# Loading the first batch's x a pair or two earlier, and taking its four differences one per pair

## Chip, cores, metric

One core of one Trainium2 chip. The time is the device time of an execution in microseconds (us). Executions of one kernel mostly agree within some 0.2% here (before: 904.19 to 905.55).

## The reference

Hash attention on (4, 8, 768, 64) inputs, then a feed-forward of 2048 with a learned leak:

```python
q_bucket = bucket(q @ proj > 0);  k_bucket = bucket(k @ proj > 0)
scores = where(q_bucket == k_bucket, q @ k.T / sqrt(D), -1e9)
attn = exp(scores - max);  attn /= sum(attn) + 1e-9
x = (attn @ v) -> (B*S, H*D)                # 3072 x 512
h = x @ w_in
out = (max(h, 0) + alpha * min(h, 0)) @ w_out
```

## The kernel before

The attention walks 16 pairs of heads (0 to 15, four to a batch). For each pair TensorE (PE) does the scores (twelve cells of six matmuls), the hash of the next pair, the turns of the pair after it (transposes of q and k), attend (weights times v) and the row sums. ScalarE (ACT) does the exponentials. VectorE (DVE) adds up the exponentials (accp, accd), divides, and rounds one piece of the weights after another in between. Each pair's x goes to DRAM. The products of the feed-forward need seven operands x0 to x6 of a batch: x0, x1, x2, x5 are loaded from DRAM, and x3, x4, x5, x6 are made as differences on DVE.

```python
def load_x(b, *ns):                       # ns: 0 -> x0, 1 -> x1, 2 -> x2, 3 -> x5
    ...
    pinned(b == 0, nc.sync.dma_start(t, x_s[b, ...]))

def sum_x(b, n, engine):                  # one difference, 128x768 fp32
    to, a, c = ((3, 5, 0), (5, 2, 5), (4, 2, 3), (6, 4, 1))[n]
    ...
    do(engine.tensor_tensor(x_m[b, to], x_m[b, a], x_m[b, c], op=ALU.subtract))

def divide(pi, between=lambda: None):
    ...
    for g in range(NCH):
        do(DVE.transpose(a[:, g], sums[pi][:, g, :HW2]))        # L800, st <- sm: frees the sums' PSUM
    do(DVE.tensor_scalar(r, ...)); do(DVE.reciprocal(...)) ...   # and four small copies on POOL
    between()                                                    # weight work and accp
    do(DVE.transpose(d, ...))                                    # dn
    do(DVE.scalar_tensor_tensor(x, av[pi], vsum[pi], d, ...))    # x: frees attend's PSUM
    nc.sync.dma_start(x_s[b, hp], x)

for pi in range(NPAIR):
    i = 2 * pi
    def weight_begin():
        weight_clamp(i); weight_parts(i); add_first(pi)          # add_first: accp
    scores(pi, ...)                                              # PE, ACT
    if pi: divide(pi - 1, weight_begin)
    ...                                                          # weight piece i
    add_third(pi); add_last(pi)                                  # accp, accd
    weight_parts(i + 1); weight_sum(i + 1); ...
    add_total(pi)                                                # accd complete
    weight_sums(2)
    ...                                                          # hash, turns
    attend(pi); totals(pi)                                       # PE; totals: sm <- accd
    ...
    if pi + 2 < NPAIR: load(pi + 2, "v")
    if pi in (9, 11, 15): load_w(...)
    if pi in (10, 12, 13):
        load_x(0, *{10: (0,), 12: (1, 3), 13: (2,)}[pi])
    if pi in (13, 14):
        for n in range(2):
            sum_x(0, 2 * pi - 26 + n, DVE)
```

Scores, hashes, turns and sums share three buffers in PSUM, the memory that PE writes its products to. `do` keeps the program's order on each engine; which buffer a tile gets is settled when the program is built, from a model of the times. What stands at the end of the loop's body (loads, differences) runs around the start of the next pair's scores: the differences of pair 13 delay pair 14.

Of the kernel before, what the change touches and what calls it, by code (L numbers as in the profile page):

```python
# [406 lines left out]
def fast_path(  # L407
# [35 lines left out]
    PE, DVE, ACT, POOL = nc.tensor, nc.vector, nc.scalar, nc.gpsimd  # L443
# [117 lines left out]
    def load_weight(i):  # L561
        if i < NW:
            i = order[i]
            raw[i] = pool.tile([P, 512], moe_w_in.dtype, name=f"raw{i}", tag="raw", bufs=3)
            nc.sync.dma_start(raw[i], piece(i))
# [17 lines left out]
    def weight_clamp(i):  # L583
        if i < NW:
            i = order[i]
            x = wx[i]
            do(DVE.tensor_scalar(x, x, HI_MIN, None, op0=ALU.max, op1=ALU.max, accum_out=wmax[:, i : i + 1]))

    def weight_parts(i):
        i = order[i]  # L590
        lo, hi = halves(i)
        x = wx[i]
        wr[i] = r = pool.tile([P, 512], F32, name=f"wr{i}", tag="wr", bufs=1)
        do(DVE.tensor_scalar(
            x.bitcast(U32), x.bitcast(U32), 3, 0xC0000000, op0=ALU.logical_shift_left, op1=ALU.bitwise_xor,
        ))
        do(DVE.tensor_scalar(r.bitcast(U32), x.bitcast(U32), 0x7F800000, None, op0=ALU.bitwise_and))
        do(DVE.scalar_tensor_tensor(r, lo, 2.0 ** -52, r, op0=ALU.mult, op1=ALU.mult))

    def weight_sum(i):  # L600


        i = order[i]
        lo, hi = halves(i)
        x, r = wx[i], wr[i]
        if i < HW:
            n, m = divmod(i, 4)
            if m == 0:
                wst[n] = pool.tile([P, NM, 4, P], F32, name=f"wsi{n}", tag="wsi")
            slot = (0, 5, 1, 2)[m]  # L610
            dst = wst[n][:, slot].rearrange("p i f -> p (i f)")
        else:
            n, m = divmod(i - HW, 2)
            if m == 0:
                wst[HW + n] = pool.tile([P, 4, DM // 2], F32, name=f"wso{n}", tag="wso")
            w = wst[HW + n]
            dst = w[:, 0:4:3] if m == 0 else w[:, 1:3]
        turned = i < HW and m == 3
        do(DVE.scalar_tensor_tensor(
            r, x, -1.0 if turned else 1.0, r, op0=ALU.mult, op1=ALU.subtract if turned else ALU.add,  # L620
        ))
        if i >= HW:
            hi, r = (t.rearrange("p (a f) -> p a f", a=2) for t in (hi, r))
        do(DVE.scalar_tensor_tensor(
            dst.bitcast(U32), hi, 0x80000000, r.bitcast(U32), op0=ALU.bitwise_and, op1=ALU.bitwise_xor,
        ))
# [99 lines left out]
    def scores(pi, cells):  # L726
        for kc, g in cells:
            sc = two_banks(f"sc{pi}_{kc}_{g}")
            ks = slice(kc * P, (kc + 1) * P)
            qs = slice(g * CW, (g + 1) * CW)  # L730
            for what, first in ((bits, True), (tr, False)):
                for s in range(2):
                    r = slice(D * s, D * s + D)
                    do(PE.matmul(  # L734
                        sc[:, s, :CW], what["k", pi][r, ks], what["q", pi][r, qs], start=first, stop=not first,
                    ))
            do(ACT.activation(pts[kc][:, g, :, :CW], sc[:, :, :CW], AF.Exp, scale=SCALE / DOWN))  # L737
# [5 lines left out]
    def add_first(pi):  # L743
        accp[pi] = pool.tile([P, 2 * NCH, CW], F32, name=f"accp{pi}", tag="accp", bufs=1)
        do(DVE.tensor_tensor(accp[pi], p(0), p(1), op=ALU.add))  # L745
        if pi:
            nc.gpsimd.dma_start(accp[pi][:, 2:], p(2)[:, 2:], accum_op=ALU.add)
# [6 lines left out]
    def add_third(pi):  # L754
        n = 2 if pi else 4
        do(DVE.tensor_tensor(accp[pi][:, :n], accp[pi][:, :n], p(2)[:, :n], op=ALU.add))

    def add_total(pi):
        do(DVE.tensor_tensor(accd[pi], accd[pi], accp[pi], op=ALU.add))  # L759
# [29 lines left out]
    def divide(pi, between=lambda: None):  # L789



        b, hp = pairs[pi]
        n = HW2 // 32
        a = pool.tile([P, NCH, HW2], F32, name=f"st{pi}", tag="st", bufs=1)
        r = pool.tile([P, NCH, n], F32, name=f"rc{pi}", tag="rc")
        rr = pool.tile([P, NCH, 2, n], F32, name=f"rr{pi}", tag="rr")
        d = pool.tile([P, NCH, CW], F32, name=f"dn{pi}", tag="dn", bufs=1)
        for g in range(NCH):
            do(DVE.transpose(a[:, g], sums[pi][:, g, :HW2]))  # L800
        do(DVE.tensor_scalar(r, a.rearrange("p g (n w) -> p g n w", w=32)[:, :, :, 0], S * EPS, None, op0=ALU.add))
        for h in range(2):
            do(DVE.reciprocal(rr[:, :, h], r))
        for q0 in (0, D):
            q1 = q0 + 32
            do(POOL.tensor_copy(rr[q0 : q0 + 32, :, 1], rr[q1 : q1 + 32, :, 1]))
            do(POOL.tensor_copy(rr[q1 : q1 + 32, :, 0], rr[q0 : q0 + 32, :, 0]))
        vsum[pi] = pool.tile([P, 1], F32, name=f"vs{pi}", tag="vs")
        do(DVE.tensor_scalar(vsum[pi], av[pi][:, 0, CW : CW + 1], EPS, None, op0=ALU.mult))
        between()  # L810
        do(DVE.transpose(
            d.rearrange("p g w -> p (g w)"),
            rr.rearrange("p g h n -> p (g h n)").unsqueeze(2).to_broadcast([P, 2 * NCH * n, 32]),
        ))

        x = mid.tile([P, NCH, CW], F32, name=f"x{pi}", tag="x", bufs=1)
        do(DVE.scalar_tensor_tensor(x, av[pi][:, :, :CW], vsum[pi], d, op0=ALU.add, op1=ALU.mult))
        nc.sync.dma_start(x_s[b, hp], x.rearrange("p g w -> p (g w)"))
# [4 lines left out]
    def pinned(when, ins):  # L823

        if when:
            do(ins)

    def load_x(b, *ns):
        for n in ns or range(4):
            m, kh, ch = ((0, 0, 0), (1, 1, 0), (2, 1, 1), (5, 0, 1))[n]  # L830
            t = mid.tile([P, 2, CW], F32, name=f"x{b}_{m}", tag=f"x{m}", bufs=1)
            pinned(b == 0, nc.sync.dma_start(
                t, x_s[b, 2 * kh : 2 * kh + 2].rearrange("k p s -> p k s")[:, :, ch * CW : (ch + 1) * CW],
            ))
            x_m[b, m] = t

    def sum_x(b, n, engine):

        to, a, c = ((3, 5, 0), (5, 2, 5), (4, 2, 3), (6, 4, 1))[n]
        if to != 5:  # L840
            x_m[b, to] = mid.tile([P, 2, CW], F32, name=f"x{b}_{to}", tag=f"x{to}", bufs=1)
        do(engine.tensor_tensor(x_m[b, to], x_m[b, a], x_m[b, c], op=ALU.subtract))
# [291 lines left out]
# [4 lines that stand above are left out]
            weight_clamp(i)  # L1138
            weight_parts(i)
            add_first(pi)  # L1140

        scores(pi, [c for c in CELLS if pi or c not in ahead])
        if pi:
            divide(pi - 1, weight_begin)
        else:
            add_first(pi)
        weight_sum(i)
        weight_group(i)
        load_weight(i + 3)
        if pi == 0:  # L1150
            weight_abs(1, DVE)
        weight_clamp(i + 1)
        add_third(pi)
        add_last(pi)
        weight_parts(i + 1)
        weight_sum(i + 1)
        weight_group(i + 1)
        load_weight(i + 4)
        add_total(pi)
        weight_sums(2)  # L1160
        if pi + 1 < NPAIR:
            hash_bits(pi + 1)
        if pi + 2 < NPAIR:
            turn(pi + 2, "q")
            turn(pi + 2, "k")
        attend(pi)
        if pi + 1 == NPAIR:
            now = ff1(0, 0)
            now.step(1)
        totals(pi)  # L1170
        if pi + 1 == NPAIR:
            now.step(5)
            divide(pi)
        else:
            weight_abs(i + 2)
        if pi + 2 < NPAIR:
            load(pi + 2, "v")
        if pi in (9, 11, 15):
            load_w((9, 11, 15).index(pi))
        if pi in (10, 12, 13):  # L1180
            load_x(0, *{10: (0,), 12: (1, 3), 13: (2,)}[pi])
        if pi in (13, 14):
            for n in range(2):
                sum_x(0, 2 * pi - 26 + n, DVE)
        if pi == 1:
            setup_alpha()
        for name in "qk":
            magnitude(pi, name)
            if pi + 3 < NPAIR:
                load(pi + 3, name)  # L1190
        if pi + 1 < NPAIR:
            weight_abs(i + 3)
# [97 lines left out]
```

## Time and profile before

| | before |
|---|---|
| time, median | 904.83 us (904.19 to 905.55, 6 runs) |
| PE busy, granted clock | 98%, 0.993 |
| DVE busy | 84% |
| sums of pair 12 to sums of pair 13 | 20.61 us |
| sums of pair 13 to sums of pair 14 | 28.74 us |
| sums of pair 14 to sums of pair 15 | 19.97 us |

The last three are differences of the start times of the groups `sm<-accd` in PE's timeline. In this text "pair 14" as a length always means the second of them. The view by stretches gives the engines' busy time in the three (columns: stretch, length, busy time of PE, weight load, DVE, ACT, POOL with instruction counts; clock; DMA share; GB/s):

```profile
278.27:298.88 20.61, 20.61 (x216) 10.37 (x212) 18.96 (x30) 18.05 (x27) 2.07 (x5) 1.00 0.69 196
298.88:327.62 28.74, 22.03 (x205) 10.26 (x198) 20.01 (x31) 16.73 (x25) 2.06 (x5) 0.88 0.59 167
327.62:347.59 19.97, 19.97 (x189) 9.52 (x189) 19.25 (x29) 9.69 (x12) 2.07 (x5) 1.00 0.25 67
```

PE fills the first and the third. In the second it lacks 6.7 us and part of its 22.0 busy us is at the lower clock. DVE, with 20.0 busy of 28.74, has a hole of its own.

### The profile page before, as it was taken

Reading aid. Unit: us, or ns where it says so; the run is one execution under the profiler, and the core shown is the slowest. Engines: PE = TensorE matmul, PEld = TensorE weight load, DVE = VectorE, ACT = ScalarE, POOL = GpSimd, SP = SyncE. Lnnn points to the kernel's source line nnn. Section 1 sums busy time; section 2 is a strip of 40 time slices with the busy share of each in tenths; the row PEclk is TensorE's granted clock in tenths of the full one; section 3 lists DMA queues with packets and bytes.
Section 4 is the critical chain, followed back from the end, with each engine's and each line's share of the span. In section 5 each row is a group of like instructions: output and inputs, shape, how many; then the busy total and the mean of one; then the engine's idle time right before and its main releaser. Section 6 shows DMA issues by size and latency. Waiting matters only on the chain.

```text
span 903.5 us, 15371 instructions
## 1 busy us (share of the span) xinstructions
PE 884.9 (98%) x5886; PEld 594.9 (66%) x5886; DVE 756.4 (84%) x1266; ACT 407.5 (45%) x726; POOL 46.3 (5%) x109
## 2 busy tenths in 40 slices
PE   8999999999999799999999999999999999999996
PEld 4444455555454345557997557998557998556996
DVE  6888989889989697899988668989768989768985
ACT  7888888888888582222112222112222111222111
POOL 0000001001000001120000000000000000000000
PEclk9999999999999899999999999999999999999998
DMA  8555686677896544578342526242436242430242
GB/s 232 138 157 135 166 242 162 168 223 201 213 266 180 163 100 159 202 262 292 141 156 83 168 100 192 94 157 82 158 110 192 94 158 78 156 117 0 94 155 59
DMA packets 124978, 140.17 MB, mean 155 GB/s; under 512 B 77776, under 2 KB 109024, under 8 KB 121312
## 3 DMA queue, kind: packets, MB, share of 16 engines
q1 hardware_dynamic: 116368, 123.90, 44.1%
q0 software_dynamic: 6384, 14.29, 6.3%
q10 hardware_dynamic: 2144, 0.92, 0.4%
q8 instruction: 48, 0.79, 0.4%
q14 instruction: 34, 0.28, 0.1%
HBM read 104.87 MB, written 28.31 MB: 147 GB/s over the span
## 4 chain that ended last, share of the span: by engine, by line
PE 88%; DVE 5%; DMA 4%; issue 2%; SPq 1%; POOL 0%; ACT 0%; DVEq 0%; ACTq 0%; POOLq 0%
PE sc L734 17%; PE av L770 13%; PE f_0a L870 2%; PE z_3a L870 2%; PE z_6a L870 2%; PE z_5a L870 2%; PE f_2a L870 2%; PE f_1a L870 2%; PE z_2a L870 2%; PE f_3a L870 2%; PE z_7a L870 2%; PE z_1a L870 2%; PE z_4a L870 2%; PE f_7a L870 2%; PE f_6a L870 2%; PE f_5a L870 2%
## 5 line engine op out<-in xcount | busy, mean ns | idle before, releaser
L737 ACT ACTIVATE pt<-sc 128x768 f32<-128x768 f32 x192 | 155.0, 812 | 47.5 <-PE sc L734 47.3
L734 PE MATMUL sc<-qT,kT 64*128 64x384 f32 x768 | 157.0, 487 | 0.0
L770 PE MATMUL av<-pt,vn 128*32 128x385 f32 (+1 forms) x1536 | 127.4, 486 | 0.0
L770 PEld LDWEIGHTS av<-pt,vn 128*32 128x32 f32 x1536 | 48.7, 109 | 71.1 <-issue 69.9
L734 PEld LDWEIGHTS sc<-qT,kT 64*128 64x128 f32 x768 | 69.1, 189 | 38.6 <-issue 38.6
L923 DVE TENSOR_TENSOR g<-g,g 128x384 f32<-128x384 f32 x128 | 68.4, 554 | 2.2
L734 PE MATMUL sc<-qb,kb 64*128 64x384 bf16 x384 | 63.6, 326 | 6.1 <-DVE st L800 5.6
L987 DVE TENSOR_TENSOR gs<-g,gs 128x768 f32<-128x768 f32 x56 | 53.3, 952 | 1.0
L979 DVE TENSOR_TENSOR ws<-wl 128x512 f32<-128x512 f32 x56 | 38.5, 687 | 17.7 <-DMA wl<-w_out_s 16.0
L987 DVE TENSOR_TENSOR gs<-g 128x768 f32<-128x768 f32 x56 | 53.3, 951 | 0.0
L734 PEld LDWEIGHTS <-kb 64*128 64x128 bf16 x384 | 19.5, 95 | 35.7 <-issue 12.6
L919 DVE SCALAR_TENSOR_TENSOR g<-h,alpha 128x384 f32<-128x384 f32 x32 | 19.7, 616 | 26.2 <-ACT h L912 26.2
L745 DVE TENSOR_TENSOR accp<-pt,pt 128x1536 f32<-128x1536 f32 x16 | 28.1, 1758 | 9.9 <-ACT pt L737 9.8
L712 ACT ACTIVATE qb<-hs,hb 32x384 bf16<-32x384 f32 x60 | 34.4, 574 | 1.1 <-PE hs L704 0.2
L752 DVE TENSOR_TENSOR accd<-accd,pt 128x1536 f32<-128x1536 f32 x16 | 28.1, 1759 | 1.7
L751 DVE TENSOR_TENSOR accd<-pt,pt 128x1536 f32<-128x1536 f32 x16 | 28.0, 1752 | 0.0
L759 DVE TENSOR_TENSOR accd<-accd,accp 128x1536 f32<-128x1536 f32 x16 | 28.0, 1750 | 0.0
L723 ACT ACTIVATE kb<-hs,hb 64x384 bf16<-64x384 f32 (+1 forms) x45 | 26.0, 578 | 0.6
L870 PE MATMUL f_0a<-x,wi 128*128 128x384 f32 x64 | 23.5, 489 | 0.0
L870 PE MATMUL f_5a<-x,wi 128*128 128x384 f32 x64 | 23.3, 486 | 0.0
L870 PE MATMUL f_6a<-x,wi 128*128 128x384 f32 x64 | 23.3, 486 | 0.0
L870 PE MATMUL f_7a<-x,wi 128*128 128x384 f32 x64 | 23.3, 486 | 0.0
(351 smaller groups left out, 1775.0 us busy)
## 6 DMA issues: line engine op xcount, KB each, us to landing
wi<-w_in_s SPq DMA_DIRECT2D x32, 896.0 KB, 4.8
wl<-w_out_s SPq DMA_DIRECT2D x16, 1024.0 KB, 4.8
wl<-w_out_r SPq DMA_DIRECT2D x12, 1024.0 KB, 4.9
raw<-in_moe_w_out_dram SPq DMA_DIRECT2D x16, 512.0 KB, 4.6
raw<-in_moe_w_in_dram SPq DMA_DIRECT2D x16, 512.0 KB, 4.6
w_in_s<-wsi SPq DMA_DIRECT2D x16, 448.0 KB, 5.7
vn<-in_v_dram SPq DMA_DIRECT2D x16, 384.0 KB, 5.0
x_s<-x SPq DMA_DIRECT2D x16, 384.0 KB, 4.4
```

Source lines behind the costliest of these rows:

```text
L712: do(ACT.activation(bits["q", pi][D * s : D * s + 32, cols], ps["q"][c : c + 32, 0 if engine is DVE else half, :CW], AF.Sign, bias=hb[c : ...
L734: do(PE.matmul(sc[:, s, :CW], what["k", pi][r, ks], what["q", pi][r, qs], start=first, stop=not first,))
L737: do(ACT.activation(pts[kc][:, g, :, :CW], sc[:, :, :CW], AF.Exp, scale=SCALE / DOWN))
L745: do(DVE.tensor_tensor(accp[pi], p(0), p(1), op=ALU.add))
L751: do(DVE.tensor_tensor(accd[pi], p(3), p(4), op=ALU.add))
L752: do(DVE.tensor_tensor(accd[pi], accd[pi], p(5), op=ALU.add))
L759: do(DVE.tensor_tensor(accd[pi], accd[pi], accp[pi], op=ALU.add))
L770: do(PE.matmul(av[pi][D * s + t : D * s + t + 32, g, :w], nat["v", pi][:, s, kc * D + t : kc * D + t + 32], pts[kc][:, g, s, :w], start=(k ...
L870: do(PE.matmul(self.ps[bank], self.left(left, k), self.right(right, k), start=start and k == 0, stop=k == self.nk - 1, skip_group_check=no ...
L923: do(DVE.tensor_tensor(new_g(b, to)[:, i], g_m[b, x][:, i], g_m[b, y][:, i], op=ALU.subtract))
L979: do(DVE.tensor_tensor(t, w2[b, n, x], w2[b, n, y], op=op))
L987: do(DVE.tensor_tensor(t, g2[b, n, x], g2[b, n, y], op=ALU.subtract))
```

## The change

Each x is loaded earlier (x0 in pair 9, x1 and x5 in pair 10, x2 in pair 12), and each pair from 12 on makes one difference whose operands were loaded at least a pair before. Number and size of all instructions stay.

```diff
-        if pi in (10, 12, 13):
-            load_x(0, *{10: (0,), 12: (1, 3), 13: (2,)}[pi])
-        if pi in (13, 14):
-            for n in range(2):
-                sum_x(0, 2 * pi - 26 + n, DVE)
+        if pi in (9, 10, 12):
+            load_x(0, *{9: (0,), 10: (1, 3), 12: (2,)}[pi])
+        if pi >= 12:
+            sum_x(0, pi - 12, DVE)
```

## The prediction

> **What bounds the kernel now.** I read the page first. TensorE (PE) is busy 98% of the 903.5 us span and is 88% of the chain that ended last, so the time is PE's work plus PE's waits, and a change can only pay by taking a wait away from PE (or can cost by adding one). The waits of PE come next, longest first:
>
> ```profile
> PE sc L734 <- DVE st L800: 5.6, 1, 5.6
> PE nil L514 <- DVE hb L518: 1.2, 1, 1.2
> PE tp_q L676 <- DMA qn<-in_q_dram: 1.0, 1, 1.0
> PE sm L784 <- DVE accd L759: 0.8, 1, 0.8
> ```
>
> The columns are total us, times, longest. There is one large wait in the whole kernel: once, 5.6 us, for the transposes that read the row sums of one pair (st<-sm). The kernel walks 16 pairs (0 to 15); the chain in order of time shows where each pair's scores start (258.50 is pair 12, 279.11 pair 13, 299.72 pair 14, 328.47 pair 15):
>
> ```profile
> 279.11 9.80 PE sc L734 x72
> 288.91 0.81 PE hs L704 x16
> 289.71 0.81 PE tp_q L676 x6
> 290.52 0.66 PE tp_k L676 x6
> 291.17 7.89 PE av L770 x96
> 299.07 0.65 PE sm L784 x16
> ...
> 303.68 4.75 DMA x<-x_s
> ```
>
> Pair 13 is an undisturbed pair: 20.61 us with no gap. In pair 14 the chain leaves PE and runs through the load of x. VectorE's (DVE) timeline there:
>
> ```profile
> 298.00 1.41 DVE L644 TENSOR_TENSOR wsi<-wsi 128x512 f32<-128x512 f32 x2
> 299.33 0.95 DVE L842 TENSOR_TENSOR x<-x,x 128x768 f32<-128x768 f32 x1
> 308.52 0.96 DVE L842 TENSOR_TENSOR x<-x,x 128x768 f32<-128x768 f32 x1 [8.24 <-DMA x<-x_s]
> 309.40 0.64 DVE L800 STREAM_TRANSPOSE st<-sm 128x192 f32<-128x192 f32 x2
> ```
>
> The second difference of pair 13 (x5 <- x2 - x5) needs x2, whose load the program places just ahead of it in the same pair. DVE takes its instructions in order, so it stands idle 8.24 us, and behind it stands the transpose that frees the PSUM buffer of the sums; PE runs out of PSUM buffers. The sync queue's timeline tells why the load was that late:
>
> ```profile
> 299.44 3.00 SPq L649 DMA_DIRECT2D w_in_s<-wsi  x3
> 302.54 1.10 SPq L487 DMA_DIRECT2D vn<-in_v_dram  x1
> 303.68 0.50 SPq L832 DMA_DIRECT2D x<-x_s  x1
> ```
>
> Three weight stores and a v load are issued ahead of it, and from its issue to landing are 4.75 us more. The stretches of the stall, PE alone (busy, granted clock, DMA share, GB/s):
>
> ```profile
> 304.53:310.09 5.56, 0.00 (x1) 0.78 0.83 239
> 310.09:314.68 4.59, 4.59 (x18) 0.52 0.00 0
> 329.23:333.82 4.59, 4.59 (x38) 1.00 0.02 4
> ```
>
> After the 5.56 us of idle PE has a clock of 0.52 for 4.59 us and gets three score cells done (18 matmuls, six a cell); the same length of time in pair 15 holds 38 at clock 1.00.
>
> **What the Trainium skill says.** "TensorE: Matmul & The Clock Gate", section "What's actually happening": the clock falls to half after an idle window of about 3.4 us and comes back after about 3.4 us of sustained work. The trace agrees in kind: 0.52 after 5.56 us idle, back to 1.00 by 314.68, so the slow stretch here is 4.59 us rather than 3.4. "VectorE: DVE Perf Modes", section "The perf-mode tier table": an fp32 tensor_tensor has only the 1x mode, whatever its operands. The trace has 0.95 us for each 128x768 difference; the change leaves its size alone. "Perfetto Trace Analysis", section "DMA Instruction — HWDGE (DVE, Sync)": the profiled length of a DMA instruction ends before the data has moved. Agreed: the x2 load's issue is 0.50 us, its landing 4.75 us after it began. So the load has to be judged by landing.
>
> **The change part by part.** Nothing is added or removed: four loads of 384 KB and four differences of 0.95 us, before and after. They move. Loads: x0 from pair 10 to 9, x1 and x5 from 12 to 10, x2 from 13 to 12. Differences: two in pair 13 and two in pair 14 become one in each of 12, 13, 14, 15.
>
> (a) The late wait. x2 is now issued at the end of pair 12, where the sync queue issued x1 and x5 at 280.58. With 4.8 us to landing (median of the x loads) it lies in SBUF at about 285.4; the difference that needs it comes at about 299.3. Margin 14 us, so the 8.24 us of DVE idle goes. All other operands land a pair or more ahead as well.
>
> (b) What PE gets back in pair 14. Pair 14 hashes but no longer turns q and k, so its PE work is 9.80 scores + 0.81 hash + 7.89 attend + 0.65 sums = 19.15 us. It took 328.47 - 299.72 = 28.75. The excess is 9.60: 5.6 of idle; about 2.2 of slow clock (4.59 for three cells of 0.81, 2.4 at full speed); 0.3 twice in the score cells that took turns on two PSUM buffers while the sums held the third; and some 0.9 at the end, where the sums waited for accd (with the slower sums).
>
> (c) What stays. In pair 14 DVE is nearly as long as PE. In pairs 13 and 15 alike accp starts 4.29 us after the first score (283.40 - 279.11; 332.76 - 328.47), held there by ScalarE's exponentials, and the DVE chain from accp to the end of accd takes 14.6 us more with the weight work in it, so accd ends 18.9 to 19.0 after the start of the pair. PE would be through attend at 18.50. So PE waits about 0.6 us for accd (0.14 of it for the signal), then runs the sums in 0.86 as it did after such a wait: 19.10 + 0.86 = about 19.96 for pair 14. Pair 15, which has the same DVE chain and took 19.97 to the end of its sums, says the same. Saved: 28.75 - 19.96 = **8.8 us**.
>
> (d) What the differences cost where they go. In pair 12 the weight differences end at 278.80 and sums' transpose starts at 279.17 after 0.37 of waiting; 0.95 in between (about 0.87 in effect, since DVE instructions overlap by some 0.08) starts it at about 279.67, 0.5 late. The buffer is then free at 280.3, before the third score cell of pair 13 at 279.11 + 2 x 0.81 = 280.7. DVE then idles 0.76 before accp in pair 13 (283.40), so the 0.5 dies there. Pair 14 starts in the same way, its two differences reduced to one ahead of pair 15; in pair 15 before, a start 0.78 late stopped no score cell. In pair 15 the last difference falls behind the division, at 352.7 in the old times, ahead of the first additions of f_0; DVE waits 0.72 us for ScalarE two instructions later, so about 0.15 us is left over, and the product that needs x6 comes some 3 us after. I count zero for PE.
>
> (e) Loads earlier by a pair or two move 0.39 MB into pairs 9 and 10. Pair 10 is the fullest for DMA (share 0.95 against 0.69 in pair 13), but q, k and v are loaded pairs ahead and no DMA wait of PE shows there: zero.
>
> Sum: 904.6 - 8.8 = **895.8 us**, 1.0% faster; no DVE or PE total changes but for PE's slow matmuls.
>
> **The rivals.**
> 1. The wait moves instead of going. For it: pair 14 is within half a microsecond of being DVE-bound, and DVE is in order, so any delay ahead of accp beyond 0.4 us comes out at accd one for one; also PSUM buffers can be dealt out anew, and cells in turns on two of them cost 0.33 each time. Against: pair 15 ran its twelve cells in 9.80 with a start 0.78 late. If two or three such losses of 0.5 to 1 us arise in pairs 12 to 15, the time is 897 to 898.
> 2. The load is hidden anyway. If DVE's stall were covered by work that PE has, only the small part on PE's path would return. For it: 8.24 us of DVE idle became only 5.6 of PE idle. Against: the chain passes through this load, the excess of pair 14 over its work is larger than the stall, and the clock loss hangs on it. If the slow clock came from something other than the idle, only 6 to 6.6 would return: about 898.3.
> 3. DVE is not the bound of pair 14 in the end: if accp could start before 4.29, or DVE's chain closes up in the shorter pair, the whole 9.60 returns: 895.0. Against: pair 15's own accd end.
> 4. The earlier loads push a weight or v load back in pair 10, and the first pairs of the feed-forward or the weight chain wait: 1 us or more lost there. Against: weight pieces land 4 to 7 us after issue and are used some 9 us after.
>
> **Range and chances.** The mean of these, weighed, lies close to 895.8: rival 3 pulls 0.8 below, rivals 1, 2 and 4 up to 2.5 above. With runs of before spread over 904.2 to 905.6, I take 894.7 to 897.8. Faster by over 2% would need 18 us, and pair 14 has 9.6 to give: 0.01. Slower by 2% would need a new stall larger than the old: 0.01. Within 2%: 0.98.
>
> **What would show it.** Right: no idle of DVE for x<-x_s in the attention; x2's load issued in pair 12's end; pair 14 (start of scores to start of scores) at about 20.0 us with clock 1.00; PE's wait for st gone and its wait for accd still there at 0.4 to 0.8; pairs 12, 13 and 15 within 0.2 of before; feed-forward blocks of unchanged length. Wrong: a PE wait for ScalarE's pt or for st in pairs 13 to 15, a pair 10 longer than 20.6, or a slow clock in pair 14 with no idle ahead of it.

## The result

| | before | after |
|---|---|---|
| time, median | 904.83 us (6 runs) | 896.13 us (895.74 to 897.08, 6 runs) |
| ratio of fast runs | 1 | 0.9905 (95%: 0.9892 to 0.9918) |
| pair 14 | 28.74 us | 19.96 us |

The ratio is the mean time of one kernel's fast runs over the mean of the other's, so it is not quite the ratio of the medians; in the experiments below the first, profiled run of each side is left out of it. The interval is well clear of 1.

The same three stretches after the change, from the view by stretches:

```profile
278.80:299.40 20.60, 20.60 (x216) 10.40 (x212) 19.73 (x31) 18.07 (x27) 2.06 (x5) 1.00 0.63 175
299.40:319.36 19.96, 19.34 (x205) 9.02 (x198) 19.12 (x30) 16.66 (x25) 2.07 (x5) 1.00 0.76 221
319.36:339.34 19.98, 19.98 (x189) 9.54 (x189) 18.39 (x28) 9.69 (x12) 2.06 (x5) 1.00 0.24 66
```

Only the middle one has changed: 8.78 us less, clock 1.00. (The spans of the two profiles differ by 8.3. The sums of pair 12 started at 278.27 before and 278.80 after, 0.53 later already; across all profiles here that start lies between 277.6 and 278.8, with the loads in the old places or the new ones, so none of it need be the change.) PE's waits after it, longest first:

```profile
PE nil L514 <- DVE hb L518: 1.2, 1, 1.2
PE z_2c L870 <- DVE m L1008: 0.8, 1, 0.8
PE sm L784 <- DVE accd L759: 0.6, 1, 0.6
```

The wait for st has gone from the list; the one for accd in pair 14 is still there with 0.6. DVE's timeline at the same place:

```profile
298.52 1.41 DVE L644 TENSOR_TENSOR wsi<-wsi 128x512 f32<-128x512 f32 x2
299.85 0.95 DVE L842 TENSOR_TENSOR x<-x,x 128x768 f32<-128x768 f32 x1
300.72 0.64 DVE L800 STREAM_TRANSPOSE st<-sm 128x192 f32<-128x192 f32 x2
...
304.53 1.76 DVE L745 TENSOR_TENSOR accp<-pt,pt 128x1536 f32<-128x1536 f32 x1 [0.35 <-ACT pt L737]
```

One difference, no wait, and the transposes directly behind it. The queue of the sync engine shows x2's load a pair earlier, 19 us ahead of its reader:

```profile
280.25 0.70 SPq L487 DMA_DIRECT2D vn<-in_v_dram  x1
281.00 0.46 SPq L832 DMA_DIRECT2D x<-x_s  x1
```

### The profile page after: what moved, and what is told of

Read it like the earlier page. It is cut to its first block, busy times and chain, and to the rows that moved or that the text cites. A ratio compares the mean times of both kernels' runs of the same rounds, so it can differ in the third digit from the quotient of the medians.

```text
span 895.2 us, 15372 instructions
## 1 busy us (share of the span) xinstructions
PE 883.6 (99%) x5886; PEld 595.2 (66%) x5886; DVE 756.2 (84%) x1266; ACT 407.2 (45%) x726; POOL 46.2 (5%) x109
## 4 chain that ended last, share of the span: by engine, by line
PE 90%; DVE 4%; DMA 3%; issue 2%; ACT 1%; SPq 1%; POOL 0%; DVEq 0%; ACTq 0%; POOLq 0%
PE sc L734 17%; PE av L770 13%; PE f_0a L870 2%; PE z_5a L870 2%; PE z_6a L870 2%; PE z_3a L870 2%; PE f_1a L870 2%; PE f_2a L870 2%; PE z_7a L870 2%; PE z_2a L870 2%; PE f_3a L870 2%; PE z_4a L870 2%; PE z_1a L870 2%; PE f_5a L870 2%; PE f_7a L870 2%; PE f_4a L870 2%
## 5 line engine op out<-in xcount | busy, mean ns | idle before, releaser
L734 PE MATMUL sc<-qT,kT 64*128 64x384 f32 x768 | 155.2, 483 | 0.0
L870 PE MATMUL f_2a<-x,wi 128*128 128x384 f32 x64 | 23.3, 487 | 0.0
```

The lines of the kernel that those rows point to most:

```text
L734: do(PE.matmul(sc[:, s, :CW], what["k", pi][r, ks], what["q", pi][r, qs], start=first, stop=not first,))
L870: do(PE.matmul(self.ps[bank], self.left(left, k), self.right(right, k), start=start and k == 0, stop=k == self.nk - 1, skip_group_check=no ...
```

## The experiments

Every experiment gave a correct result. The lengths of pair 14 and the start of accp are from each one's own profile; all timed runs were in the fast state, the two single looks are of unknown state.

| kernel | median us | ratio to before | accp starts after sums 13 | pair 14 | difference |
|---|---|---|---|---|---|
| before | 904.83 | 1 | 13.89 | 28.74 | 14.85 |
| after | 896.13 | 0.9905 | 5.13 | 19.96 | 14.83 |
| x2_load_only | 896.48 | 0.9907 | 5.76 | 20.59 | 14.83 |
| x2_late_again | 904.60 | 0.9991 | 13.98 | 28.80 | 14.82 |
| difference_later | 896.82 | 0.9904 | 5.13 | 19.97 | 14.84 |
| wait_behind_transpose | 903.85 | 0.9995 | 12.55 | 27.37 | 14.82 |
| repeat_2 | 898.28 (one look) | - | 6.74 | 21.60 | 14.86 |
| repeat_3 | 898.80 | 0.9934 | 8.68 | 23.50 | 14.82 |
| repeat_5 | 901.11 (one look) | - | 9.69 | 24.52 | 14.83 |
| repeat_9 | 904.73 | 0.9998 | 13.63 | 28.49 | 14.86 |
| transpose_late | 900.40 | 0.9948 | 5.46 | 23.07 | 17.61 |
| total_first | 895.83 | 0.9903 | 5.13 | 19.14 | 14.01 |

The last column is the key to all of them: from the start of accp to the sums pass 14.82 to 14.86 us in the ten kernels that leave the DVE work between accp and the sums alone, wherever PE stops in these runs. (The last two rows change that work itself.) In repeat_3 and repeat_5 it was close: no wait for accd is listed there, PE came to the sums less than 0.1 us ahead of accd, and a longer stop of PE could have set the length.

### x2_load_only: one load moved, nothing else

```diff
-        if pi in (10, 12, 13):
-            load_x(0, *{10: (0,), 12: (1, 3), 13: (2,)}[pi])
+        if pi in (10, 12):
+            load_x(0, *{10: (0,), 12: (1, 3, 2)}[pi])
```

> Kernel before with one thing moved: x2 is loaded in pair 12 behind x1 and x5; the differences stay two in pair 13 and two in pair 14. Theory (the late load is the cause): the 8.2 us wait of VectorE is gone; but the two differences in a row start pair 14's division some 1.4 us after the scores, so accp starts 0.6 us later than in the changed kernel and the end of accd with it: 896.7 us, 0.9% faster than before. Rival (the spreading of the differences is what pays): about 904 to 905. Rival (spread is worth nothing): equal to the changed kernel, 896.1.

896.48 us (ratio 0.9907, 0.989 to 0.9923); no wait for x. Pair 14 takes 20.59, 0.63 over the changed kernel, because two differences in a row start the transposes 1.0 us later against the sums (301.31 - 298.99, after the change 300.72 - 299.40), of which 0.35 is taken up by what was DVE's wait for the exponentials ahead of accp. So of the 8.78 us the load gives 8.15 and the spreading 0.63; in the total the 0.63 can't be told from noise.

### x2_late_again: the load put back

```diff
-        if pi in (9, 10, 12):
-            load_x(0, *{9: (0,), 10: (1, 3), 12: (2,)}[pi])
+        if pi in (9, 10, 13):
+            load_x(0, *{9: (0,), 10: (1, 3), 13: (2,)}[pi])
```

> The changed kernel with one thing undone: x2 is loaded in pair 13 again, so the difference of pair 13 asks for it at once. Theory: the wait is back, 8 us of VectorE idle ahead of the difference, pair 14 at 28 to 29 us, 904.5 to 905.3 us, though x0, x1, x5 come earlier and the differences are spread. Rival (spreading or the other loads pay): 897 to 900.

904.60 us (0.9991, 0.9974 to 1.0008). The DVE timeline has the wait again:

```profile
308.49 0.96 DVE L842 TENSOR_TENSOR x<-x,x 128x768 f32<-128x768 f32 x1 [9.19 <-DMA x<-x_s]
```

The earlier loads of x0, x1, x5 and the spread differences are worth nothing as long as this one load is late.

### difference_later: loads untouched, the reader moved

```diff
-        if pi in (13, 14):
-            for n in range(2):
-                sum_x(0, 2 * pi - 26 + n, DVE)
+        for n in {13: (0,), 14: (1, 2), 15: (3,)}.get(pi, ()):
+            sum_x(0, n, DVE)
```

> Kernel before with all loads where they were; the difference that reads x2 goes from pair 13 to pair 14 (order: one in 13, two in 14, one in 15). Theory (only the distance from load to reader counts, not where the load stands): no wait for x, 895.9 to 896.4 us as in the changed kernel. Rival (the load must be earlier because of the traffic of pair 13): over 900.

896.82 us (0.9904, 0.9887 to 0.992), and pair 14 within 0.01 of the changed kernel's. The two differences of pair 14 both read x2 here, and neither waits:

```profile
318.94 1.82 DVE L842 TENSOR_TENSOR x<-x,x 128x768 f32<-128x768 f32 x2
```

The load may stay where it was, in the traffic of pair 13; what counts is that its reader does not come right behind it.

### wait_behind_transpose: DVE still waits, PE's buffer is freed first

```diff
-        if pi in (13, 14):
-            for n in range(2):
-                sum_x(0, 2 * pi - 26 + n, DVE)
+        for n in {13: (0,), 14: (2, 3)}.get(pi, ()):
+            sum_x(0, n, DVE)
...
         def weight_begin():
+            if pi == 14:
+                sum_x(0, 1, DVE)
             weight_clamp(i)
```

> Kernel before, loads unmoved; the difference that waits for x2 goes behind the division's two transposes, reciprocals and the sum of v in pair 14, ahead of the weight work and accp. So VectorE still waits for x2 until about 308.5 in the profile, but the PSUM buffer of the sums is freed at once and PE has no reason to stop in the scores. Theory A (the prediction's own split: PE's stop for the PSUM buffer, 5.6 us, and its slow clock, 2.2 us, are what the time was lost to): 896.5 to 898.5 us. Theory B (VectorE's lateness runs on through accp and accd to the sums, and the stop and the slow clock lie beside it): accp starts only some 1.1 us earlier than before, PE waits for VectorE in attend and in the sums instead, 903 to 904 us.

903.85 us (0.9995, 0.9976 to 1.0014; one of its four runs was 906.67). The DVE timeline shows the transposes freed and the wait kept:

```profile
300.15 0.64 DVE L800 STREAM_TRANSPOSE st<-sm 128x192 f32<-128x192 f32 x2
...
308.24 0.96 DVE L842 TENSOR_TENSOR x<-x,x 128x768 f32<-128x768 f32 x1 [6.88 <-DMA x<-x_s]
```

PE now runs all twelve score cells of pair 14 in a row at full clock, and yet nearly nothing is gained. PE's timeline shows where it stands instead:

```profile
315.12 10.18 PE L770 MATMUL av<-pt,vn 128*32 128x385 f32 x96 [4.85 <-DVE x L817]
326.19 0.86 PE L784 MATMUL sm<-accd,ones 128*32 128x192 f32 x16 [0.89 <-DVE accd L759]
```

Attend waits for the buffer that pair 13's x frees, starts at the low clock (10.18 instead of 7.96 us), and even so is done 0.89 before accd. Pair 14 is 1.37 shorter than before; accp starts 1.34 earlier. This is theory B: pair 14 is as long as DVE's lateness makes it, and PE's stop and slow clock lie beside that.

### repeat_2, repeat_3, repeat_5, repeat_9: lateness without a transfer

The changed kernel with the first difference, whose result stays the same, done again k times in pair 13:

```diff
+        if pi == 13:
+            for n in range(k):
+                do(DVE.tensor_tensor(x_m[0, 3], x_m[0, 5], x_m[0, 0], op=ALU.subtract))
         if pi >= 12:
             sum_x(0, pi - 12, DVE)
```

> The changed kernel with the first difference done three times more ahead of pair 13's own difference (same result, no transfer): VectorE is 2.6 us later into pair 14. Theory (VectorE's lateness comes out at accd): 0.35 us of it is taken up by the wait ahead of accp, 2.3 us come out, 898.4 us; PE stops for the PSUM buffer little or not at all and its clock stays at 1.00. Rival (only the PSUM buffer matters, lateness under 4 us is hidden because five score cells can run on two buffers): 896.1 to 897.

> The same with nine repeats: VectorE 7.9 us later with no transfer in it. Theory (lateness of VectorE of whatever origin is the cost): 0.35 is taken up, 7.5 us come out, 903.6 us; PE idles about 4.5 to 7 us in the scores and its clock falls to about half after it. Rival (the cost came from the DMA traffic or the wait for a transfer): under 900.

repeat_9: 904.73 us (0.9998, 0.9982 to 1.0015), pair 14 28.49, 8.53 over the changed kernel. Nine repeats bring the kernel back to where it was, with no late load in it. 7.5 were expected, from a pitch of 0.88 us; these repeats, which all write one tile, follow at 0.99:

```profile
298.69 8.90 DVE L1184 TENSOR_TENSOR x<-x,x 128x768 f32<-128x768 f32 x9
```

The lateness comes out one for one: the difference of pair 13 starts 8.93 us later than in the changed kernel (against the sums), 0.35 is taken up by DVE's wait ahead of accp, and 8.53 come out. repeat_3: 898.80 us (0.9934, 0.9918 to 0.9951), pair 14 3.54 over, where 2.3 were expected. Here PE does come in, which the expectation had as good as excluded: the third score cell was given the sums' buffer, and PE stood 2.43 us. Its timeline (the middle is left out):

```profile
303.58 0.34 PE L734 MATMUL sc<-qb,kb 64*128 64x384 bf16 x2 [2.43 <-DVE st L800]
303.75 0.96 PE L734 MATMUL sc<-qT,kT 64*128 64x384 f32 x4
...
304.83 1.49 PE L734 MATMUL sc<-qT,kT 64*128 64x384 f32 x4
```

The fourth cell's exponential came late by that and by the slow clock, and accp waited 0.92 us for it (2.97 later, less 0.35, plus 0.92 is 3.54). So PE's stop can reach the path, by delaying what DVE needs next. The other two doses were looked at once, to see where the clock falls:

> Two repeats ahead of pair 13's difference. PE waits about 1.5 us for the PSUM buffer of the sums (third score cell, as with three repeats). If the clock needs an idle stretch of more than 2 us to fall, the score cells behind it keep 0.81 us each and pair 14 takes VectorE's lateness: 19.96 + 2.0 - 0.35 = 21.6 us. If it falls here too: 1.5 us idle and about 1.2 to 1.6 of slow clock against PE's 19.15: 22 to 22.3 us.

> Five repeats, 4.9 us later. Theory (VectorE's lateness comes out at accd, less 0.35): 24.4 to 24.6 us for pair 14. PE waits some 2.5 to 4.4 us in the scores, depending on whether the cells run on two buffers, and its clock falls after it.

Pair 14 took 21.60 and 24.52 us, as expected. The same place in PE's timeline, repeat_2:

```profile
302.69 0.34 PE L734 MATMUL sc<-qb,kb 64*128 64x384 bf16 x2 [1.43 <-DVE st L800]
302.87 0.81 PE L734 MATMUL sc<-qT,kT 64*128 64x384 f32 x4
```

and repeat_5:

```profile
305.35 0.50 PE L734 MATMUL sc<-qb,kb 64*128 64x384 bf16 x2 [3.26 <-DVE st L800]
305.62 1.51 PE L734 MATMUL sc<-qT,kT 64*128 64x384 f32 x4
```

After 1.43 us of idle the four float32 matmuls of a cell take 0.81 us as ever; after 3.26 they take 1.51 from the first cell on.

### transpose_late: the buffer freed late, accp on time

```diff
-        if pi:
+        if pi == 14:
+            weight_begin()
+            divide(pi - 1)
+        elif pi:
             divide(pi - 1, weight_begin)
```

> The changed kernel with pair 14's division put behind the weight work and accp: the PSUM buffer of the sums is freed at about 6.7 us into the pair instead of 1.1, while accp starts at its usual 4.3. Score cells run on two buffers to about 4.9 us, then PE idles some 1.8 us[...]. The division's two transposes and small operations (1.2 us) now lie between accp and accd, so accd ends 1.2 us later: the pair takes 21.2 to 21.7 us and the kernel 897.3 to 897.9. If PE's stop did not count at all, 897.3; if the clock fell too, 899 or more.

900.40 us (0.9948, 0.9931 to 0.9964): 2.5 us more than expected, and not for the reason under test. PE waited only 0.23 us for the buffer. But the division has four small copies on POOL in its middle, and with nothing between them and their reader DVE stood 1.56 us:

```profile
308.38 0.98 DVE L811 STREAM_TRANSPOSE dn<-rr 128x768 f32<-128x768 f32 x1 [1.56 <-POOL rr L807]
```

That and the 1.2 us of the division itself now lay between accp and accd (17.61 instead of 14.83), PE waited 2.33 us ahead of the sums, and its clock fell once more: the sums took 1.51 us, and pair 15 took 21.50 us (19.98 in the changed kernel). The run shows what stands on the path, but it does not separate PE's stop from the rest.

### total_first: what is left in pair 14

```diff
+        if pi == 14:
+            add_total(pi)
         weight_parts(i + 1)
         weight_sum(i + 1)
         weight_group(i + 1)
         load_weight(i + 4)
-        add_total(pi)
+        if pi != 14:
+            add_total(pi)
```

> The changed kernel, and in pair 14 the last addition into accd ahead of the second weight piece's parts and sum (3.0 us of VectorE work that no sums wait for). Theory (what is left in pair 14 is VectorE's chain to accd): PE's wait of 0.6 us for accd goes, the sums take 0.65 instead of 0.86, pair 14 takes 19.15 instead of 19.97 us; VectorE is 0.7 us late into pair 15, which the kernel before took without loss. 895.3 us, 0.8 us under the changed kernel. Rival (VectorE's total over the pairs 14 and 15 bounds, so the gain comes back in pair 15): 896.1.

895.83 us (0.9903, 0.9887 to 0.992). The view by stretches has pair 14 and pair 15:

```profile
298.99:318.13 19.14, 19.14 (x204) 9.10 (x200) 18.30 (x28) 16.07 (x24) 2.07 (x5) 1.00 0.74 214
318.13:338.09 19.96, 19.96 (x192) 9.49 (x185) 19.20 (x30) 10.41 (x13) 2.07 (x5) 1.00 0.29 83
```

PE fills both; the wait for accd is gone, and pair 15 gives nothing back. Because 0.8 us does not show against the spread of whole runs, the two were run once more on one chip:

> The changed kernel once more, on the same chip and in the same rounds as the next one, because 0.8 us is to be told apart: 896.1 us, 19.96 us from the sums of pair 13 to the sums of pair 14.

> total_first once more. Its profile had pair 14 at 19.14 us, 0.82 under the changed kernel, and pair 15 unchanged; its total was not clear of the changed kernel's. If the 0.8 us are kept: 895.3 us, ratio to the kernel before 0.9895 against 0.9904 for the changed kernel. Rival (they are given back in the feed-forward): no difference.

897.09 us (895.97 to 897.52; 0.9909) against 895.30 us (894.53 to 897.88; 0.9901), four runs each; their intervals overlap. Pair 14 took 19.96 and 19.15 us. Shown: 0.8 us less in the stage, twice. Not shown clear of noise: the gain in the total, though the order was the expected one both times. Its medians are the lowest of the versions run.

## Why the prediction was right

**(a) The late wait** was right. x2's load is issued at 281.00, its reader starts at 299.85 and does not wait; x2_late_again and difference_later show that it is the distance between the two that counts.

**(b) What PE gets back** had the right total (its four parts as listed add up to 9.3) and a wrong split. The 9.60 us of excess were put down to 5.6 of PE idle, 2.2 of slow clock, the cells on two buffers and 0.9 ahead of the sums, as if each were lost and regained. They do fill the time, but they did not set it: wait_behind_transpose takes the first three out of the scores, PE waits in attend instead, and 27.37 of 28.74 us remain. The length was set by DVE: x2 lands, difference, division, accp at 13.89, and 14.85 us of DVE work from there to the sums. PE's stop and slow clock filled time that PE would have waited for accd anyway; that remaining wait of 0.8 us in the list of before was the sign, since it says that PE was still ahead of DVE after all its losses. The chain that ended last, which the prediction quotes only as far as the load of x, says it outright in the profile before: from the load it runs on through DVE to the sums, and PE's stop is not on it (start, length; parts left out):

```profile
308.52 0.96 DVE x L842
309.48 0.57 DVE st L800 x2
...
312.86 1.67 DVE accp L745
...
325.71 1.77 DVE accd L759
327.48 0.14 issue
327.62 0.86 PE sm L784 x16
```

The prediction's own rival 1 (delay ahead of accp "comes out at accd one for one") has the mechanism that the repeats then showed.

**(c) What stays** was right and carried the number: accp held at 4.29 us after the first score by the exponentials, then the DVE chain, hence 19.96 us for pair 14. Measured 19.96, with the 0.6 us wait for accd. total_first shows that this rest is DVE's order and can be had.

**(d) The moved differences** cost PE nothing, as predicted: pairs 13 and 15 took 20.60 and 19.98 us (20.61 and 19.97 before). The one in pair 15 left no trace some microseconds on: the four differences of g in f_0 start 11.45 us after the sums of pair 15 both before (359.04 - 347.59) and after (350.79 - 339.34).

**(e) The earlier loads** fill the DMA engines further in the stretch behind pair 10 (share 1.00, before 0.95). It holds PE's work of pair 11, though the prediction calls it pair 10, and is 20.61 us long, as before (20.60).

**Rivals.** 1, moved waits: none in the changed kernel, but repeat_3 shows the form it takes, accp waiting for an exponential that a stopped PE delivered late. 2, a hidden load, fell; its working (6 to 6.6 us come back if the slow clock has another cause) rested on the wrong split, as the slow clock was not on the path. 3, the whole 9.60, fell by the 0.6 wait and the slower sums behind it. 4 did not occur: from the sums of pair 15 to the end of the span it is 555.9 us before and after. The predicted 895.8 missed the median by 0.3 us: 8.8 against 8.78 measured in the stage. Of the 0.3, 0.2 is the starting value (904.6, where the median is 904.83), the rest is within noise. The number was not luck: it came from (c), DVE's chain, and did not need the split in (b).

## What to carry to other kernels

On an engine that works in order, an instruction that reads a transfer must stand a transfer's landing time plus the queue ahead of it away from the load; here one 384 KB load placed just ahead of its reader cost 8.2 us of 905 (what x2_load_only got back in pair 14). A long wait on the busiest engine names the place, not yet the size: ask which wait would end the stage if that one were gone, and follow the late engine's own chain to the stage's end. Where two engines are both nearly full in a stage, look at the order of the follower's work too: here an addition moved forward was worth 0.8 us in a stage of 20.

## What the Trainium skill lacked or had wrong

- "TensorE: Matmul & The Clock Gate", section "What's actually happening", lets the clock fall after an idle window of about 3.4 us. Here it fell after shorter idle: 2.33 us (transpose_late) and 2.43 us (repeat_3), and not after 1.43 us (repeat_2). After 2.43 us the slow stretch did not begin with the restart but some 0.9 us later. An estimate from the mean granted clock of the wait, taken as 1.0 until the fall and 0.5 from there: the fall came 3.1 us into the wait of before (0.78 over 5.56 us) and 2.2 us into that of transpose_late (0.96 over 2.34 us). Why less than the page's window was enough, no run here shows. The page lets the clock come back after about 3.4 us of work; slow stretches here were 4.59 us after 5.56 of idle and some 3.1 after 3.26. The low clock of one half agrees (granted 0.52 before).
- "Perfetto Trace Analysis", section "Optimization Strategy", has one find the gaps of the most-contended engine and what blocks them. It lacks the check that the next wait in the same stage would end as late: taking away the block of this kernel's longest gap (5.6 us) alone gave 1.37 us.
- The same page, section "DMA Instruction — HWDGE (DVE, Sync)", was borne out (issue 0.50 us, landing 4.75 us). It follows one DMA instruction, after which the sequencer is free for the next, and does not add up what a load waits for those ahead of it: of the 8.24 us that DVE waited, from 300.28 on, 3.4 had passed when the load was issued at 303.68, behind three weight stores and a v load.
